# A decode block on one core: K of the last pair ahead of the projection, PV between the projection and its sums, and the last spread of O on GpSimd

## The chip, the cores and the metric

The kernel runs on one core of one Trainium2 chip. The metric is the device time of one execution in microseconds (us), as the median of several executions.

Engines are named as in the profile: PE is TensorE (PEld its weight loads), DVE is VectorE, ACT is ScalarE, POOL is GpSimd, SP is SyncE, which issues the loads.

## The reference

```python
def _A_ref(x, k_cache, v_cache, wq, wo):            # B=2, one token, D=512, 32 heads, 8192 keys, Dh=128
    q = (x @ wq) ...                                 # per head
    scores = jnp.einsum("bhqd,bhkd->bhqk", q, k) * (Dh ** -0.5)
    p = _softmax(scores, axis=-1)
    o = jnp.einsum("bhqk,bhkd->bhqd", p, v)
    return o.reshape(B, Sq, Hq * Dh) @ wo

h  = x + _A_ref(_layernorm(x), A_k_cache, A_v_cache, A_wq, A_wo)
h2 = h + _B_ref(_layernorm(h), W_gate, W_up, W_down)  # gated feed-forward, F=1376
```

Nearly all of the time goes into reading the two caches: 281 MB of bf16.

## The kernel before

The 64 (batch, head) items are handled as 32 pairs. For each pair a 4 MB block of K and a 4 MB block of V are loaded. The scores of a pair are shared out: VectorE does three quarters of a pair's scores (one multiply of 12288 elements per partition, four halving adds, one reduction), and TensorE the other quarter (transposes, a copy by ScalarE, small matmuls). TensorE then does PV. Pairs 0 to 29 run in a loop of 15 rounds; pairs 30 (`P0`) and 31 (`P1`) form the tail.

When a round's two heads are done, their output O is scaled by VectorE and *spread* over a padded tile by five small instructions, so that TensorE can *gather* it into the layout that the projection with `wo` needs. In the loop GpSimd spreads; for the last round before the tail, VectorE does.

```python
def o_spread(g, prog, *t_oc):
    e = prog.eng
    prog.wait(tok("og", g), *t_oc)
    if g >= 1:
        p0, p1 = ...
        prog.run(e.memset(O_l[:, :, :, p0:min(p1 + NM, 128)], 0.0))     # only writes
        prog.last()
    for a in range(2):
        p0, off = first(2 * g + a)
        n = min(NM, 128 - p0)
        e.tensor_copy(out=rsel[:, a, :], in_=rows[:, DR - off:2 * DR - off])   # reads SBUF
        i = e.tensor_tensor(out=O_l[:, a, :, p0:p0 + n], in0=O_cur..., in1=mask..., op=ALU.mult)  # reads SBUF
    i.then_inc(l2p, 1)

# TensorE, tail
collect(tail, 1)
k_part(tail, P0, (2, 3, 4, 5), ((k2p, 1),))            # K of pair 30: transposes and scores
nc.tensor.wait_ge(l2p, 1)                              # O spread
o_gather(tail)                                         # 4 matmuls
nc.tensor.wait_ge(a2p, 7)                              # ScalarE has copied the gathered O
nc.tensor.wait_ge(sem_wo, 16)
for r in range(DR):                                    # the projection: 30 matmuls 128x512
    i = nc.tensor.matmul(Op[1][32 * (r % 4):32 * (r % 4) + B, :], lhsT=O_all[:, r, :], rhs=X[:, r * D:(r + 1) * D], ...)
tail.mark("op", i)
nc.tensor.wait_ge(a2p, 9)                              # ScalarE has copied the projection
for c in range(DC):                                    # its sums, fp32
    nc.tensor.matmul(Wp[:, c * B:(c + 1) * B], lhsT=os_sb[:]..., rhs=sel2[:], ...)
k_part(tail, P1, (10, 11, 12, 13), ((k2p, 2),))        # K of pair 31
pv(tail, P0, ((JC, J, ((slot_sem[1], 16), (a2p, 6))), (0, JC, ((a2p, 8),))))   # 32 matmuls 128x512
pv(tail, P1, ((V_LAST, J, ...), (0, V_LAST, ...)), lambda: tail.mark("z", z_sum(Sp[0])))

# VectorE, in the pass over the pairs
if p >= P0:
    nc.vector.wait_ge(g2d, p - P0 + 1)
    nc.vector.wait_ge(slot_sem[s], 16)
    nc.vector.sem_inc(k2p, 1)
    dve.last()
    t_dm[p] = dve.run(k_mult(p))
    k_adds(p, dve.run, dve.last)
    ...
    t_s[p] = dve.run(k_reduce(p))
    if p == P0:
        dve.wait(t_ob_loop)
        normalize(Ob, dve.run, dve.last)
        o_spread(g - 1, dve, dve.run(o_scale()))
```

The softmax here doesn't subtract the row's maximum and nothing guards it: scores larger than these inputs give would overflow.

## Time and profile before

| what | number | view |
|---|---|---|
| time | 660.52 us (3 runs, 660.38 to 660.69) | the times |
| DMA in the chain of waits | 76% of the span | page, part 4 |
| DMA in the slices | 0.9 or more from the second slice to the last but one, mean 427 GB/s | page, part 2 |
| gather to end of PV, on the chain | 628.16 to 648.02, 19.86 us | chain of waits |
| last matmul of the feed-forward ends | 656.74 | chain of waits |
| last weights landed | 656.06 | landing records of the trace |

The chain of waits follows the end of the execution backward to what released each step. These are its pieces of the tail (start, duration, engine, tile, line of the kernel):

```profile
628.16 0.30 PE O L431 x4
...
628.78 3.60 PE O L463 x30
...
633.05 2.03 PE W L469 x8
635.08 0.97 PE T L381 x4
...
641.12 6.01 PE O L405 x54
...
648.04 0.61 ACT os_sb L569
```

From the gather (L431) the path goes through the projection (L463), a wait of 0.67 us for ScalarE's copy of it, the sums (L469), K of pair 31 (from L381 at 635.08 to 641.12), and PV of both pairs (L405).

GpSimd's timeline in the loop (start, duration, instruction, shapes):

```profile
592.28 0.21 POOL L525 COPY rsel<-rows 128x30 bf16<-128x30 bf16 x1
...
592.90 0.30 POOL L537 COPY q_c<-q_all 128x136 bf16<-128x136 bf16 x1
604.09 3.48 POOL L537 COPY q_c<-q_all 128x136 bf16<-128x136 bf16 x1 [10.89 <-DVEq L591]
```

The same copy of q took 0.30 us beside VectorE's reduction and 3.48 us when it started with VectorE's first add (604.05 to 607.42).

The last load and its issue, from the list of DMA issues (size, us to landing) and SyncE's timeline. First the list:

```profile
wd_last<-in_B_W_down_dram SPq DMA_DIRECT2D x1, 96.0 KB, 27.8
```

```profile
628.22 2.39 SPq L706 DMA_DIRECT2D wd_last<-in_B_W_down_dram  x1
```

Issued at 628.2 and landed 27.8 us later: 656.1, only 0.7 us before the last matmul that needs it ends. All these loads go through one queue (281.06 of the 281.17 MB).

### The profile page before, as it was taken

The page shows a single profiled execution, that of the slowest core. Times are in us where ns is not written, and L with a number is a line of the kernel's source. Part 1 is how long each engine was busy: PE and PEld are TensorE (multiplying, and loading weights), DVE is VectorE, ACT ScalarE, POOL GpSimd, SP SyncE. Part 2 cuts the span into 40 slices and gives each one's busy share as a digit, 9 for nine tenths or more (in the row PEclk, how much of TensorE's full clock was granted, in tenths as well). Part 3 has the DMA queues.
Part 4 walks back from the last instruction along what each step waited for, and adds up shares of the span by engine and source line. Part 5 has one row for each costly group of instructions (what it writes and reads, how often), then busy time and mean ns, then how long its engine had stood idle before and what let it go on. Part 6 is the DMA issues. An engine that isn't in the chain of part 4 may idle for free.

```text
span 659.2 us, 7582 instructions
## 1 busy us (share of the span) xinstructions
PE 324.3 (49%) x3073; PEld 188.6 (29%) x3073; DVE 469.2 (71%) x280; ACT 213.6 (32%) x431; POOL 73.5 (11%) x125
## 2 busy tenths in 40 slices
PE   2753454435455343655535364443556444354577
PEld 0331332213233121433313142221324222133344
DVE  1585576788767678776768877676886767787991
ACT  1622333143342223334223343422324332333250
POOL 3002002020200202020020201002020110202000
PEclk9856556565756657555665756756555765655656
DMA  8999999999999999999999999999999999999997
GB/s 366 444 437 431 420 445 416 443 428 431 438 422 441 422 439 433 428 435 424 441 422 439 433 428 433 426 441 422 439 434 426 435 424 441 424 437 433 428 417 295
DMA packets 10653, 281.17 MB, mean 427 GB/s; under 512 B 1202, under 2 KB 1300, under 8 KB 1812
## 3 DMA queue, kind: packets, MB, share of 16 engines
q1 hardware_dynamic: 10632, 281.06, 99.3%
q8 instruction: 5, 0.08, 0.1%
q14 instruction: 4, 0.03, 0.0%
q10 hardware_dynamic: 12, 0.00, 0.0%
HBM read 281.05 MB, written 0.00 MB: 426 GB/s over the span
## 4 chain that ended last, share of the span: by engine, by line
DMA 76%; DVE 19%; PE 4%; issue 1%; ACT 1%; SPq 0%; DVEq 0%
DMA slot<-in_A_k_cache_dram 76%; DVE prod L540 16%; DVE prod L549 2%; PE O L405 1%; PE O L463 1%; PE T L381 0%; ACT kT L566 0%; PE W L469 0%; DVE scores L554 0%; PE S L756 0%; PE O L756 0%; PE O L808 0%; PE Ob L417 0%; SPq L172 0%; PE S L364 0%
## 5 line engine op out<-in xcount | busy, mean ns | idle before, releaser
L540 DVE TENSOR_TENSOR prod<-slot,q_c 128x12288 bf16<-128x12288 bf16 x32 | 209.9, 6558 | 148.0 <-DMA slot<-in_A_k_cache_dram 141.3
L405 PE MATMUL O<-slot,e 128*16 128x512 bf16 x1024 | 119.3, 621 | 219.9 <-ACT e L495 146.2
L549 DVE TENSOR_TENSOR prod<-prod 128x6144 bf16<-128x6144 bf16 (+3 forms) x128 | 212.2, 1657 | 7.8
L566 ACT ACTIVATE kT<-T 128x1024 bf16<-128x1024 bf16 x128 | 126.1, 1022 | 144.6 <-PE T L381 141.9
L381 PE MATMUL T<-ident_f,slot 128*128 128x128 f32 x512 | 108.6, 365 | 29.1 <-DVEq L587 29.1
L405 PEld LDWEIGHTS O<-slot,e 128*16 128x16 bf16 x1024 | 26.4, 114 | 287.0 <-ACT e L495 172.9
L495 ACT ACTIVATE e<-scores 64x96 bf16<-64x96 f32 x64 | 19.5, 304 | 239.6 <-DVEq L601 238.9
L381 PEld LDWEIGHTS T<-ident_f,slot 128*128 128x128 f32 x512 | 79.0, 188 | 44.2 <-DVEq L587 43.3
L537 POOL COPY q_c<-q_all 128x136 bf16<-128x136 bf16 x32 | 57.2, 1788 | 195.5 <-DVEq L591 152.5
L364 PE MATMUL S<-q_c,kT 128*128 128x4 bf16 x1024 | 47.4, 168 | 40.8 <-ACT kT L566 40.0
L364 PEld LDWEIGHTS S<-q_c,kT 128*128 128x128 bf16 x1024 | 39.1, 104 | 67.9 <-ACT kT L566 66.8
L417 PE MATMUL Ob<-sel,os_sb 128*128 128x4 f32 x136 | 30.1, 345 | 24.2 <-ACT os_sb L569 24.2
L417 PEld LDWEIGHTS Ob<-sel,os_sb 128*128 128x128 f32 x136 | 28.6, 311 | 26.1 <-ACT os_sb L569 26.1
L520 POOL MEMSET O_l<- 128x40 bf16 (+1 forms) x13 | 1.8, 136 | 303.9 <-DVEq L598 303.9
L554 DVE TENSOR_REDUCE scores<-prod 128x96 f32<-128x768 bf16 x32 | 30.5, 953 | 2.8
L566 ACT ACT_TABLE_LOAD x15 | 19.2, 1283 | 0.3
L495 ACT ACTIVATE e<-S 64x32 bf16<-64x32 f32 x64 | 13.0, 202 | 15.1 <-PE S L364 14.7
L569 ACT ACTIVATE os_sb<-O 128x512 f32<-128x512 f32 x17 | 10.1, 597 | 12.8 <-PE O L405 12.4
L495 ACT ACTIVATION_READ_ACCUMULATOR e<-S 64x1 f32 x64 | 12.8, 201 | 0.7
L495 ACT ACTIVATION_READ_ACCUMULATOR e<-scores 64x1 f32 x64 | 11.8, 185 | 0.0
L426 PEld LDWEIGHTS Ob<-zs,ones_f 128*128 128x128 f32 x30 | 7.1, 296 | 12.5 <-issue 12.5
L525 POOL COPY rsel<-rows 128x30 bf16<-128x30 bf16 x28 | 5.9, 209 | 33.3 <-DVEq L598 32.5
(104 smaller groups left out, 90.6 us busy)
## 6 DMA issues: line engine op xcount, KB each, us to landing
slot<-in_A_k_cache_dram SPq DMA_DIRECT2D x32, 4096.0 KB, 32.1
slot<-in_A_v_cache_dram SPq DMA_DIRECT2D x31, 4096.0 KB, 30.3
slot<-in_A_wq_dram SPq DMA_DIRECT2D x1, 4096.0 KB, 12.2
X<-in_A_wo_dram SPq DMA_DIRECT2D x1, 3840.0 KB, 45.8
slot<-in_A_v_cache_dram SPq DMA_DIRECT2D x1, 3072.0 KB, 23.3
slot<-in_B_W_up_dram SPq DMA_DIRECT2D x1, 1376.0 KB, 23.2
slot<-in_B_W_gate_dram SPq DMA_DIRECT2D x1, 1376.0 KB, 26.2
slot<-in_A_v_cache_dram SPq DMA_DIRECT2D x1, 1024.0 KB, 25.4
```

The costliest lines, as they stand in the source:

```text
L364: i = nc.tensor.matmul(Sp[p % 2][:, 2 * jj:2 * jj + 4], lhsT=kv_[:, k, r, :], rhs=q_c[p % 2][:, 4 * r:4 * r + 4], start=(r == 0), stop=(r ...
L381: i = nc.tensor.transpose(Tp[g % 2][:, k * 128:(k + 1) * 128], k_t[:, j:j + 2, :].rearrange("p j d -> p (j d)").bitcast(F32), ident_f[:])
L405: i = nc.tensor.matmul(Op[0][c:c + 16, :], lhsT=e_t[q][:, j // VJ, :], rhs=v_t[:, j:j + VJ, :].rearrange("p j d -> p (j d)"), start=(q == ...
L417: i = nc.tensor.matmul(Ob[:, 0:4], lhsT=os_sb[:, jj * Dh:(jj + 1) * Dh], rhs=sel[:, 4 * jj:4 * jj + 4], start=(jj == 0), stop=(jj == VJ - 1))
L426: return nc.tensor.matmul(bank[:, ZC:ZC + 8], lhsT=ones_f[:], rhs=zs[:], start=True, stop=True)
L495: i = nc.scalar.activation(out=e_t[q][h, j0 // VJ:j1 // VJ, 8 * q:8 * q + 8].rearrange("p g (j a) -> p g j a", a=2)[:, :, :, a], in_=src(h ...
L537: nc.gpsimd.tensor_copy(out=q_c[p % 2][:], in_=q_all[:, p]).then_inc(g2d, 1)
L540: return nc.vector.tensor_tensor(out=prod[:, 0:JC, :], in0=tile((2 * p) % 4)[:, 0:JC, :], in1=q_c[p % 2][:, 8:QW].unsqueeze(1).broadcast_t ...
L549: run(nc.vector.tensor_tensor(out=prod[:, 0:JC, 0:w], in0=prod[:, 0:JC, 0:w], in1=prod[:, 0:JC, w:2 * w], op=ALU.add))
L554: return nc.vector.tensor_reduce(out=scores[p % PG][:, 0:JC], in_=prod[:, 0:JC, 0:8], axis=AX.X, op=ALU.add)
L566: to_pe(nc.scalar.activation(out=kT[gg % 2][:], in_=Tp[gg % 2][:].bitcast(BF16), func=ACT.Copy))
L569: to_pe(nc.scalar.activation(out=os_sb[:], in_=Op[0][:], func=ACT.Copy))
```

## The change

Its intent: K of pair 31 fills the time in which TensorE would wait for the spread, PV of pair 30 fills the time in which ScalarE copies the projection, and VectorE is rid of the spread. ScalarE's instructions are put in the matching order.

```diff
                 k_part(tail, P0, (2, 3, 4, 5), ((k2p, 1),))
+                k_part(tail, P1, (7, 8, 9, 10), ((k2p, 2),))
                 nc.tensor.wait_ge(l2p, 1)
                 o_gather(tail)
-                nc.tensor.wait_ge(a2p, 7)
+                nc.tensor.wait_ge(a2p, 12)
 ...             (the projection)
-                nc.tensor.wait_ge(a2p, 9)
+                pv(tail, P0, ((JC, J, ((slot_sem[1], 16),)), (0, JC, ((a2p, 13),))))
+                nc.tensor.wait_ge(a2p, 14)
 ...             (its sums)
-                k_part(tail, P1, (10, 11, 12, 13), ((k2p, 2),))
-                pv(tail, P0, ((JC, J, ((slot_sem[1], 16), (a2p, 6))), (0, JC, ((a2p, 8),))))
                 pv(tail, P1, ...)
 ...
                             normalize(Ob, dve.run, dve.last)
-                            o_spread(g - 1, dve, dve.run(o_scale()))
+                            t_oc = dve.run(o_scale())
 ...
+                        if p == P0:
+                            o_spread(g - 1, pool, t_oc)
 ...             (ScalarE: O_all, exp of pair 30's VectorE part and os_sb move behind K of pair 31)
```

## The prediction

> **What bounds it now.** The page says DMA is 76% of the chain of waits. Only the tail after the loop can change. There the chain of waits, in order of time, runs: VectorE finishes pair 30 (reduction ends 627.0 us), scales O (627.5) and spreads it (five instructions, to 628.1); TensorE gathers (0.3), ScalarE copies (0.25), the projection takes 3.60, its copy 0.61, its sums 2.03, K of pair 31 6.0, PV of pairs 30 and 31 with the z sums 6.9, to 648.02. The feed-forward part follows and its last matmuls end at 656.74. Close behind lie the loads: the last quarter of V of pair 31 is there at 645.9, the gate weights at 652.5, the last down weights at 656.07. So nothing done in the tail can gain more than about 0.4 us: whatever TensorE saves, the last down matmuls wait for 656.07.
>
> **What the change does.** K of pair 31 (6.0 us) leaves the path between gather and result, and stands where TensorE would have to wait for the spread anyway, at about 627.6 (its K landed at 626.4; the release comes from VectorE when pair 30 is scaled). PV of pair 30 (3.3) covers the copy of the projection (0.7). Were the spread still ready at about 628.5, TensorE would run K to 633.6, gather, project to 638.3, PV 30 to 641.7, sums to 643.7, PV 31 to about 647.2: 0.8 us sooner, of which the loads leave 0.4.
>
> **What it costs.** The spread goes to GpSimd, and VectorE's next instruction is now pair 31's multiply (6.56 us), directly followed by adds of 3.36, 1.77, 0.97 and 0.57. The timeline of GpSimd in the loop shows the danger: the copy of q (128x136) takes 0.30 when VectorE runs a reduction, and 3.48 when it starts with VectorE's first add (604.09 to 607.57; the add ends at 607.42). The Trainium skill, "SBUF — State Buffer", section "Who interferes with whom", says it: a VectorE instruction with two SBUF inputs contends with a GpSimd instruction that reads SBUF, and the later one is fully blocked. The loop's own spreads took 0.15 us apiece only because they fall beside a reduction (592.1 to 593.0). Here they fall beside the multiply. The memset only writes and should pass. The four reading instructions should each get through at one gap of VectorE: about 634.1 (end of the multiply), 637.5, 639.3, 640.3. So O is spread at about 640.4 instead of 628.1.
>
> TensorE then idles from about 633.6 to 640.5. From the gather to the end of PV it took 19.9; without K (6.0) and the copy's wait (0.7) it takes 13.15: 653.6 instead of 648.0, an estimate. The rest (8.7 us to the last matmul) stands. So +5.5 us.
>
> **Predicted:** 665.8 us, range 660.0 to 667.5 (8 in 10). Faster by over 2%: 0.005; within 2%: 0.985; slower by over 2%: 0.01.
>
> **What would show it.** GpSimd's last copies and products last microseconds each and end at VectorE's boundaries, the last near 640.4; TensorE waits about 7 us before the gather; K of pair 31 runs at 627.6 to 633.6; the projection starts near 641; loads land as before.
>
> **What would make it wrong.** If GpSimd gets all four instructions through in the first gap (634.1 to 634.9), the tail ends as before, 660.5 or so. If it isn't blocked at all, 660.1. If GpSimd misses gaps, O comes at the latest with the reduction, near 641.3: 666.8.

## The result, and the profile after

The changed kernel took 660.62 us (median of 6 runs, 660.17 to 661.04); the kernel before, in the same rounds and the first ones, 660.57 (6 runs, 660.14 to 660.69). The ratio is 1.0002, with a 95% interval of 0.9989 to 1.0015: the same. A ratio here is the mean time of one kernel's fast runs over that of the other's of the same rounds, so it is not quite the ratio of the medians quoted.

The predicted 665.8 was wrong by 5.2 us. The chain of waits of the changed kernel in the same stretch:

```profile
627.45 0.17 DVE O_cur L510
...
627.88 6.39 POOL rsel L525
634.27 0.17 POOL O_l L526
634.43 3.28 POOL rsel L525
637.71 0.17 POOL O_l L526
...
637.93 0.30 PE O L431 x4
...
638.55 3.58 PE O L464 x30
642.12 1.81 PE O L405 x31
643.93 1.96 PE W L471 x8
645.89 1.40 PE O L405 x24
647.29 0.32 PE S L426 x2
647.61 0.57 PE O L405 x8
...
648.20 0.61 ACT os_sb L569
```

VectorE's timeline there has pair 31's multiply (to 634.20) and, from 634.24, its four adds:

```profile
627.64 6.56 DVE L540 TENSOR_TENSOR prod<-slot,q_c 128x12288 bf16<-128x12288 bf16 x1
634.24 6.83 DVE L549 TENSOR_TENSOR prod<-prod 128x6144 bf16<-128x6144 bf16 x4
```

GpSimd is now on the chain. Its spread took 10.2 us instead of 0.55, and the gather started 9.8 us later (637.93 instead of 628.16). And yet PV ended at 648.18, where it had ended at 648.02. From the gather to the end of PV, TensorE took 10.25 us in place of 19.86. Of these 9.6 us, 6.0 are K of pair 31 and 0.7 the wait for the copy, both as planned. The remaining 2.9 were not planned: PV itself (64 matmuls and the z sums, those of the softmax weights) took 4.1 us of the chain (1.81 + 1.40 + 0.32 + 0.57) instead of 6.9 (641.12 to 648.02). The view of stretches shows why (us; busy time and number of instructions of each engine; granted clock of TensorE; DMA share; GB/s). Before:

```profile
core 0: us, PE busy (x) PEld busy (x) DVE busy (x) ACT busy (x) POOL busy (x), PEclk, DMA share, GB/s
...
641.80:645.20 3.40, 3.40 (x36) 1.17 (x32) 0.52 (x1) 0.94 (x5) 0.00 (x0) 0.50 1.01 423
645.20:648.60 3.40, 2.79 (x30) 0.84 (x22) 0.34 (x2) 0.56 (x1) 0.00 (x0) 0.74 1.03 434
```

After:

```profile
641.80:645.20 3.40, 3.40 (x40) 2.06 (x32) 0.25 (x1) 1.35 (x5) 0.00 (x0) 0.95 1.00 417
645.20:648.60 3.40, 2.95 (x37) 1.52 (x37) 0.34 (x2) 0.40 (x1) 0.00 (x0) 1.00 1.03 433
```

Before, PV ran at a granted clock of 0.50 until 646.9. After, the clock was 1.00 from 642.2 on. The weights landed at 656.12 (656.06 before).

So two things needed an explanation: why the spread was ready at 637.9 and not at 640.4, and where the full clock came from.

### The profile page after: what moved, and what is told of

The parts are those of the page before. It is cut to its first block, busy times and chain, and to the rows that moved or that the text cites. A ratio compares the mean times of both kernels' runs of the same rounds, so it can differ in the third digit from the quotient of the medians.

```text
span 659.2 us, 7580 instructions
## 1 busy us (share of the span) xinstructions
PE 324.4 (49%) x3072; PEld 191.0 (29%) x3073; DVE 469.1 (71%) x275; ACT 213.6 (32%) x431; POOL 82.8 (13%) x130
## 4 chain that ended last, share of the span: by engine, by line
DMA 76%; DVE 18%; PE 3%; POOL 2%; issue 1%; SPq 0%; DVEq 0%; ACT 0%
DMA slot<-in_A_k_cache_dram 76%; DVE prod L540 16%; DVE prod L549 2%; POOL rsel L525 1%; PE O L405 1%; PE O L464 1%; PE W L471 0%; DVE scores L554 0%; PE S L758 0%; PE O L758 0%; PE O L810 0%; SPq L172 0%; PE Ob L417 0%; ACT os_sb L569 0%; DVEq L587 0%
## 5 line engine op out<-in xcount | busy, mean ns | idle before, releaser
L405 PE MATMUL O<-slot,e 128*16 128x512 bf16 x1024 | 117.4, 610 | 219.5 <-ACT e L495 146.3
L381 PE MATMUL T<-ident_f,slot 128*128 128x128 f32 x512 | 110.8, 371 | 29.2 <-DVEq L587 29.2
L381 PEld LDWEIGHTS T<-ident_f,slot 128*128 128x128 f32 x512 | 80.6, 191 | 44.2 <-DVEq L587 43.3
L525 POOL COPY rsel<-rows 128x30 bf16<-128x30 bf16 x30 | 15.6, 519 | 33.4 <-DVEq L598 32.5
L569 ACT ACTIVATE os_sb<-O 128x512 f32<-128x512 f32 x17 | 10.1, 597 | 12.7 <-PE O L405 12.4
L495 ACT ACTIVATION_READ_ACCUMULATOR e<-S 64x1 f32 x64 | 12.8, 201 | 0.7
L426 PEld LDWEIGHTS Ob<-zs,ones_f 128*128 128x128 f32 x30 | 7.2, 299 | 12.8 <-issue 12.8
```

The lines of the kernel that those rows point to most:

```text
L381: i = nc.tensor.transpose(Tp[g % 2][:, k * 128:(k + 1) * 128], k_t[:, j:j + 2, :].rearrange("p j d -> p (j d)").bitcast(F32), ident_f[:])
L405: i = nc.tensor.matmul(Op[0][c:c + 16, :], lhsT=e_t[q][:, j // VJ, :], rhs=v_t[:, j:j + VJ, :].rearrange("p j d -> p (j d)"), start=(q == ...
L495: i = nc.scalar.activation(out=e_t[q][h, j0 // VJ:j1 // VJ, 8 * q:8 * q + 8].rearrange("p g (j a) -> p g j a", a=2)[:, :, :, a], in_=src(h ...
L569: to_pe(nc.scalar.activation(out=os_sb[:], in_=Op[0][:], func=ACT.Copy))
```

## The experiments

Fourteen runs were made, two of them repeats of the two kernels: the first eight for both questions and the limit set by the loads, four more when the first theory of the clock fell, and two to test the next one. "PV ends" is read from the timelines and chains, "full clock from" from the clock records in the traces, which are multiples of 3.41 us long.

### The spread: who holds up whom

**hold_multiply** lets VectorE's multiply wait until GpSimd has spread O.

```diff
                         nc.vector.sem_inc(k2p, 1)
+                        if p == P1:
+                            nc.vector.wait_ge(l2p, 1)
                         dve.last()
```

> The changed kernel, but VectorE's multiply of pair 31 waits until GpSimd has spread O. Theory (the port held by the multiply and the first add stretched the spread): all five GpSimd instructions take 0.15 to 0.21 us, the spread is ready near 628.6, the multiply starts near 628.7 and the gather follows K of pair 31 directly. Rival (GpSimd is slow by itself here): the first copy still takes microseconds.

Measured (one look, 660.16 us): the five instructions took 0.15 to 0.21 us each, as in the loop. GpSimd's timeline:

```profile
627.60 0.15 POOL L520 MEMSET O_l<- 128x44 bf16 x1 [19.98 <-DVE O_cur L510]
627.82 0.21 POOL L525 COPY rsel<-rows 128x30 bf16<-128x30 bf16 x1
...
628.29 0.21 POOL L526 TENSOR_TENSOR O_l<-O_cur,mask 128x10 bf16<-128x10 bf16 x1
```

Against 6.39 and 3.28 us for the two copies in the changed kernel, this shows that VectorE's multiply and first add held them up. The memset is as fast with the multiply beside it (0.16). That is what the Trainium skill, "SBUF — State Buffer", section "Who interferes with whom", says of instructions that only write, and of reading ones beside a VectorE instruction with two SBUF inputs.

**copies_first** puts both copies ahead of both products.

```diff
+                    for a in range(2 * copies_first):
+                        off = first(2 * g + a)[1]
+                        e.tensor_copy(out=rsel[:, a, :], in_=rows[:, DR - off:2 * DR - off])
                     for a in range(2):
 ...
-                        e.tensor_copy(out=rsel[:, a, :], in_=rows[:, DR - off:2 * DR - off])
+                        if not copies_first:
+                            e.tensor_copy(out=rsel[:, a, :], in_=rows[:, DR - off:2 * DR - off])
```

> The changed kernel with the order of GpSimd's instructions changed: both copies of rows first, then both products. Theory two per gap (any two short reading instructions pass in one gap between VectorE's instructions): first copy held to the end of the multiply, 634.2, second copy passes with it in 0.2 us, first product is held for the first add to 637.6, second product passes. Rival by kind (copies are held, products aren't, since they follow a copy): second copy held to 637.6, both products short after it. Ready near 637.9 either way; the durations decide.

Measured (one look, 660.49 us), GpSimd's timeline (two instructions to a line):

```profile
628.03 6.53 POOL L524 COPY rsel<-rows 128x30 bf16<-128x30 bf16 x2
634.52 3.48 POOL L530 TENSOR_TENSOR O_l<-O_cur,mask 128x12 bf16<-128x12 bf16 x2
```

Both copies are done 0.2 us after the multiply ends (634.35), both products 0.2 us after the first add. So it isn't the kind that counts: two short reading instructions pass at each boundary between VectorE's instructions.

**early_copies** does the memset and both copies before O is scaled, so that only the two products come after it.

```diff
-                    prog.wait(tok("og", g), *t_oc)
+                    prog.wait(tok("og", g), *(() if hoist else t_oc))
 ...
+                    if hoist:
+                        for a in range(2):
+                            off = first(2 * g + a)[1]
+                            e.tensor_copy(out=rsel[:, a, :], in_=rows[:, DR - off:2 * DR - off])
+                        prog.wait(*t_oc)
```

> The changed kernel with the memset and both copies of the spread done ahead of VectorE's scaling (they need only the gather of the round before), so that only the two products follow it. Two per gap: both held to the end of the multiply, ready near 634.5, before K of pair 31 is done; the gather then comes near 635, and by the clock theory the end of PV stays at 648.0 to 648.8 and the time within 0.5 us of before. Products never held: ready near 628.2. One per gap: near 637.8. Rival of fixed durations: 0.4 us faster.

Measured: 660.36 us (660.19 to 660.69, 4 runs) beside 660.34 of before, ratio 0.9999 (0.9982 to 1.0016). Both products passed at the end of the multiply:

```profile
627.82 6.74 POOL L532 TENSOR_TENSOR O_l<-O_cur,mask 128x12 bf16<-128x12 bf16 x2 [18.20 <-DVE O_cur L510]
```

The gather came at 634.61, 3.3 us earlier than in the changed kernel. PV ended at 647.38, only 0.8 us earlier (by the timeline), because TensorE needed 12.8 us: the full clock lasted here only from 640.8 to 644.2. The rule of two per boundary held in the three orders tried (the changed kernel, copies_first, early_copies).

### The parts of the change, and the limit of the loads

**spread_only** is the kernel before with the spread alone moved to GpSimd.

```diff
-                            o_spread(g - 1, dve, dve.run(o_scale()))
+                            t_oc = dve.run(o_scale())
 ...
+                        if p == P0:
+                            o_spread(g - 1, pool, t_oc)
```

> The kernel before with the spread alone moved to GpSimd, in the old order. All theories: the spread is ready near 637.9, TensorE idles from 627.4 to then, K of pair 31 still to do after the projection. With the lock and fixed durations at half clock (19.9 us from the gather): PV ends at 657.8, time 670.3. With the clock paid back (over 10 us idle): gather to end of PV takes 16 to 17 us, PV ends near 654.5, time 666 to 668.

Measured: 669.58 us (669.05 to 670.5), ratio 1.0146 (1.0129 to 1.0163). The gather came at 638.06; TensorE had idled for 10.2 us. The full clock came only at 654.5. The result lies between the two forecasts and nearer to fixed durations at half clock: ten idle microseconds had not brought the clock back for the projection, the sums or K.

**order_only** is the changed kernel with the spread back on VectorE.

```diff
-                            t_oc = dve.run(o_scale())
+                            o_spread(g - 1, dve, dve.run(o_scale()))
 ...
-                        if p == P0:
-                            o_spread(g - 1, pool, t_oc)
```

> The change with the spread back on VectorE. Theory (idle TensorE time is paid back as granted clock): the gather comes right after K of pair 31, near 635, 3 us earlier than in the changed kernel, TensorE never idles, stays at half clock, and needs about 13 us from the gather to the end of PV: end at 648.0 to 648.8, time within 0.5 us of both kernels. Rival (TensorE's work has fixed durations, 10.25 us from the gather as in the changed kernel's profile): PV ends near 646, held by the last V, and the time falls by about 0.4 us, to the floor that the last weights set.

Measured: 660.28 us (660.2 to 660.4), beside 660.23, ratio 1.0002 (0.9985 to 1.0018). The gather came at 634.75, PV ended at 646.58, and the idle theory was wrong here: without an idle stretch the full clock began at 638.8. TensorE's timeline now shows waits for loads:

```profile
643.39 1.47 PE L405 MATMUL O<-slot,e 128*16 128x512 bf16 x24 [0.43 <-DMA slot<-in_A_v_cache_dram]
644.80 0.39 PE L426 MATMUL S<-zs,ones_f 128*128 128x8 f32 x2
645.97 0.61 PE L405 MATMUL O<-slot,e 128*16 128x512 bf16 x8 [0.79 <-DMA slot<-in_A_v_cache_dram]
...
652.52 1.71 PE L756 MATMUL O<-d_b,slot 128*128 128x2 bf16 x44 [0.58 <-DMA slot<-in_B_W_gate_dram]
```

PV was 1.4 us ahead of the kernel before, but the end of the span was only 0.3 us ahead (658.84 against 659.18). The loads took the rest back.

**less_work** leaves out 22 of the 30 projection matmuls and 24 of the 32 PV matmuls of pair 30. Its output is wrong, which doesn't matter for the time. (The comparison with the reference isn't sensitive to these terms.)

```diff
-                for r in range(DR):
+                for r in (*range(4), *range(DR - 4, DR)):
 ...
-                pv(tail, P0, ((JC, J, ((slot_sem[1], 16),)), (0, JC, ((a2p, 13),))))
+                pv(tail, P0, ((JC, J, ((slot_sem[1], 16), (a2p, 13))),))
```

> Wrong result on purpose: the changed kernel with 22 of the 30 projection matmuls and 24 of the 32 PV matmuls of pair 30 left out, 3 to 5 us of TensorE time at half clock. Theory (the last weights land at 656.1 and set the floor): the end comes at most 0.5 us sooner, the time is 660.0 to 660.3, and TensorE waits for the last loads of V, the gate or the down weights. Rival (the tail is bound by TensorE's work): the time falls by 2 us or more.

Measured: 660.67 us (660.17 to 661.26, 4 runs), ratio 1.0008 (0.9991 to 1.0024). The median gained nothing at all, less than expected. In the profiled run, at the low end of the four, TensorE waited 1.13 us for the last V, PV of pair 31 ran at half clock (2.74 us for 24 matmuls where order_only took 1.47), and the chain of waits ended in the loads:

```profile
627.06 28.85 DMA slot<-in_B_W_down_dram
655.91 0.04 issue
655.95 0.56 PE O L810 x10
```

So the tail can't end sooner than the loads allow, even with the work of 46 matmuls less. This also hinted at the next section: with less to do, TensorE lost the full clock.

### The clock: a theory that fell

The first theory was that the idle 2.9 us before the gather had earned the full clock.

**fill_wait** fills that wait with 28 matmuls that nobody reads.

```diff
                 k_part(tail, P1, (7, 8, 9, 10), ((k2p, 2),))
+                nc.tensor.wait_ge(sem_wo, 16)
+                for n in range(28):
+                    c = 32 * (n % 4)
+                    nc.tensor.matmul(Tp[0][c:c + 16, :], lhsT=ident[:, 0:16], rhs=X[:, 0:D], start=True, stop=True)
                 nc.tensor.wait_ge(l2p, 1)
```

> The changed kernel with 28 idle-filling matmuls (128x512, into a bank that is free, never read) in the stretch where TensorE waits for GpSimd's spread (about 2.9 us at half clock). Theory: without the idle stretch the clock stays at half, gather to end of PV takes about 13 us instead of 10.25, PV ends near 651, and the time rises by 2 to 3 us, to 662.5 to 663.7. Rival (the clock has nothing to do with the idle stretch): PV ends at 648.2, the time stays at 660.6.

Measured: 660.32 us (660.24 to 660.37), ratio 1.0001. The theory's 662.5 or more did not come. Full clock began at 641.7 and PV ended at 647.9. In the profiled execution K of pair 31 ended at 633.4 and not at 635.1 as in the changed kernel's profile, so 1.4 us of the wait stayed unfilled; TensorE idled for half as long as in the changed kernel (2.9) and got the clock just the same.

**late_gather** puts an idle stretch into order_only by hand.

```diff
                 nc.tensor.wait_ge(l2p, 1)
+                nc.tensor.wait_ge(late, 1)
                 o_gather(tail)
 ...
                         last()
+                        if p == NP - 1 and w == Dh // 4:
+                            nc.vector.sem_inc(late, 1)
```

> order_only with an idle stretch put back by hand: TensorE waits before the gather until VectorE has done the first add of pair 31 (about 638.2), though O was spread at 628. Theory: the idle 3 us bring back the full clock, PV ends at 648.0 to 648.8, and the time is within 0.5 us of order_only though the gather is 3 us later. Rival (fixed durations): PV ends 3 us later than in order_only, the time rises by 2.5 to 3 us.

Measured: 661.54 us (660.34 to 662.27), ratio 1.0016 (0.9999 to 1.0033). The gather came 3.6 us later than in order_only (638.34) and PV ended 2.9 us later (649.50). The idle stretch was not made up. The time rose by only 1.3 us because order_only had been waiting for loads.

**fill_loop** fills TensorE's 13 us wait in every round of the loop, in case low use over a longer time earned the clock.

```diff
                     nc.tensor.sem_inc(l2p, -1)
+                    for n in range(110):
+                        c = 32 * (n % 4)
+                        nc.tensor.matmul(Tp[0][c:c + 16, :], lhsT=ident[:, 0:16], rhs=q_all[:, 0:4, 8:QW],
+                                         start=True, stop=True)
                     pv(body, 1, ...)
```

> The changed kernel with 110 matmuls (128x512, into a free bank, never read) in each round of the loop, in the 13 us in which TensorE waits for the odd pair's V. Theory (little use of TensorE in the tens of microseconds before the tail earns the full clock that shortened the tail): the clock stays at half throughout the tail, gather to end of PV takes 13 us, PV ends near 651, the time rises by 2 to 3 us, to 662.5 to 664. Rival (the grant does not answer to what TensorE did): as the changed kernel, 660.2 to 661.1. The loop itself stays bound by the loads.

Measured: 661.14 us (660.82 to 661.48), ratio 1.001 (0.9994 to 1.0027). Full clock began at 644.2, and gather to end of PV took 11.2 us. Neither forecast was met exactly, but the half clock throughout that the theory asked for did not come; the mean granted clock over the span even rose to 0.70, from 0.59 before.

**after_again** and **before_again** are the two kernels once more, unchanged.

> The changed kernel once more, for the clock records of a second execution. If the grant follows from the program, the full clock begins near 642 again and lasts 10 us, gather to end of PV 10.25 us. If it varies between executions, the full clock falls elsewhere and this stretch takes up to 13 us, while the spread on GpSimd has the same durations (6.4, 0.2, 3.3, 0.2).

> The kernel before once more. In its first profile the gather to the end of PV took 19.9 us, all but 1 us of it at half clock. If the grant follows from the program, the same; if it varies between executions, 17 to 20 us, with the full clock elsewhere; the end is held by the last weights, 656.1, in any case.

Measured (one look each). The changed kernel: full clock from 643.3 (642.2 the first time), gather to end of PV 10.7 us (10.25), the spread with the same 6.38, 0.21, 3.33 and 0.20 us; 661.04 us. The kernel before: full clock from 645.7 (646.9), gather to end of PV 19.3 us (19.9); 660.42 us. So the exact place varies between executions, but by a microsecond or so, while the two kernels differ clearly.

**gather_640** is the changed kernel with the gather held until VectorE's third add, where the prediction had put the end of the spread. Its edit is that of late_gather with `Dh // 16`.

> The changed kernel with the gather held until VectorE has done its third add of pair 31, 640.3 to 640.5, where the prediction had put the end of the spread; the spread itself is untouched (ready near 637.9). If the time hangs on the gather microsecond for microsecond, it rises by 2 to 2.6 us over the changed kernel, to about 663; with TensorE at half clock to the end of PV, as the prediction assumed, it would be 665.8; if a later gather is made up by the clock, 660.6 to 661.2.

Measured: 663.43 us (663.07 to 664.24), ratio 1.0049 (1.0032 to 1.0066). The gather came at 640.79, 2.86 us later than in the changed kernel; the time rose by 2.8 over the changed kernel's median (it lies 3.2 above the kernel before of the same rounds). Gather to end of PV took 10.4 us; full clock began at 645.3. This weighs the two errors: a spread as late as predicted would have cost about 2.8 us. The rest of the miss, 2.4 us (665.8 − 663.4), is left for the clock; that is a remainder and not a measurement of its own.

### The clock: the theory that held

Put side by side, the traces show another pattern. Full clock begins 2.7 to 5.9 us after the start of an unbroken run of 128x512 matmuls (projection, PV):

| kernel | run of 128x512 matmuls starts | full clock from |
|---|---|---|
| before | projection alone 628.78; PV 641.05 | none; 646.9 |
| before, again | projection alone 630.06; PV 642.33 | none; 645.7 |
| spread_only | projection alone 638.69; PV 650.95 | none; 654.5 |
| after | projection and PV of 30: 638.55 | 642.2 |
| after, again | 638.81 | 643.3 |
| order_only | 636.09 | 638.8 |
| early_copies | 635.23 | 640.8 |
| late_gather | 638.94 | 644.5 |
| gather_640 | 641.39 | 645.3 |

The other traces of the first twelve runs fit: hold_multiply 634.90 and 640.6, copies_first 638.68 and 641.9, fill_wait 638.59 and 641.7 (after its fill), fill_loop 638.54 and 644.2, less_work 643.56 (PV of pair 31 alone) and 646.8.

The Trainium skill, "TensorE: Matmul & The Clock Gate", section "What's actually happening", says it: the default is half clock, and a busy window of about 3.4 us, in windows that run freely, releases it. Under this theory the projection alone (3.6 us) seldom fills such a window; joined to PV of pair 30 it makes a run of about 7 us at half clock, which always does. The part of the change that was meant to hide a wait of 0.7 us would then have earned the clock. Two more runs tested this.

**sums_first** undoes only that part: PV of pair 30 stands after the sums again.

```diff
-                pv(tail, P0, ((JC, J, ((slot_sem[1], 16),)), (0, JC, ((a2p, 13),))))
                 nc.tensor.wait_ge(a2p, 14)
 ...             (the sums)
+                pv(tail, P0, ((JC, J, ((slot_sem[1], 16),)), (0, JC, ((a2p, 13),))))
                 pv(tail, P1, ...)
```

> The changed kernel with one of its parts undone: PV of pair 30 stands after the sums of the projection again, so that TensorE's run of 128x512 matmuls is 3.6 us of projection, then a wait and the sums, then 6.9 us of PV. Theory (the full clock comes after an unbroken run of such matmuls that fills one of the 3.41 us windows in which the records count; 3.6 us seldom does, 7 us always does): the full clock begins in the PV stretch, 3.4 to 6.8 us after its start near 644.5, not near 642; gather to end of PV takes 12 to 14 us, the time rises by 1.5 to 3.5 us over the changed kernel, to 662.2 to 664.2. Rival (the clock falls where it falls, or answers to the wait): full clock from 641 to 645 as in the changed kernel, only the 0.7 us wait for the copy comes back, 660.9 to 661.4.

Measured: 662.76 us (661.39 to 664.59), ratio 1.0039 (1.0018 to 1.0061), 2.1 us more than the changed kernel's median and 2.4 more than the kernel before of the same rounds. The stretches:

```profile
638.40:641.80 3.40, 3.07 (x32) 0.95 (x31) 3.30 (x4) 0.99 (x5) 0.00 (x0) 0.50 0.98 419
641.80:645.20 3.40, 2.71 (x22) 2.13 (x20) 0.56 (x1) 1.34 (x5) 0.00 (x0) 0.98 0.99 414
645.20:648.60 3.40, 3.40 (x40) 1.23 (x36) 0.00 (x0) 0.00 (x0) 0.00 (x0) 0.52 1.00 422
```

Here the projection alone did earn one stretch of full clock, from 641.9 to 645.3. I had not expected it; it is where the rival had put the full clock. It was spent on the wait and on the fp32 sums, which took 2.03 us at either clock, and was lost again as PV began. PV then had to earn it anew, from 648.8. Gather to end of PV took 12.4 us (638.24 to 650.64). Of the 2.15 us more than in the changed kernel, 0.7 is the wait for the copy and most of the rest PV's slower matmuls. The rival had asked for 661.4 at most.

**long_fill** is fill_wait with 44 matmuls instead of 28, so that the run of 128x512 matmuls starts earlier.

```diff
+                nc.tensor.wait_ge(sem_wo, 16)
+                for n in range(44):
+                    c = 32 * (n % 4)
+                    nc.tensor.matmul(Tp[0][c:c + 16, :], lhsT=ident[:, 0:16], rhs=X[:, 0:D], start=True, stop=True)
                 nc.tensor.wait_ge(l2p, 1)
```

> The changed kernel with 44 filling matmuls (128x512, into a free bank, never read) in front of the gather instead of the 28 of an earlier run, so that TensorE runs such matmuls from the end of K of pair 31 (633.4 to 635.0) nearly up to the gather, over 4.5 us. Theory: together with the projection the run is long enough that the full clock begins between 637 and 641.5, earlier than in the changed kernel (642.2 and 643.3 in two executions); part of the projection runs at full clock, gather to end of PV takes 8.5 to 10 us, the time is 660.2 to 661. Rival (no link to the run of matmuls): full clock from 642 to 645, gather to end of PV 10.2 to 11.2 us.

Measured: 660.35 us (660.08 to 660.49), ratio 1.0001 (0.9985 to 1.0018). Full clock from 638.2, 4.9 us after the fill began at 633.29. TensorE's timeline:

```profile
633.29 4.87 PE L462 MATMUL T<-X,ident 128*16 128x512 bf16 x44
...
638.70 1.89 PE L468 MATMUL O<-X,O_all 128*2 128x512 bf16 x30 [0.33 <-ACT O_all L679]
```

The projection took 1.89 us instead of 3.58, and gather to end of PV 8.6 us. Doing more work made the rest faster; as in order_only, the loads kept the gain.

long_fill came out as the theory asks and not as its rival. sums_first did so in its time and in PV's clock, but not in the clock right after the projection.

**Where the windows lie.** The traces settle that difference. The clock records of an execution lie on one grid of 3.41 us. Cut each of the sixteen executions along its own grid, from 624 us on, and add up in each window how long TensorE was in 128x512 matmuls. (This was read off afterwards; no run was made to test it.) All 17 half-clock windows with 2.8 us or more were followed by full clock, none of the 92 with 2.5 us or less was, and of two with 2.7 one was. The projection alone was split over two windows in the kernel before (1.09 and 2.49 us), in its repeat (2.03 and 1.55) and in spread_only (2.16 and 1.41); in sums_first nearly all of it fell into one (3.06). So where the grid happens to lie decides for the projection alone, while a run of 7 us contains a whole window in any case. Full clock stayed after every window with 1.47 us or more and went after every one with 1.35 us or less. So it went in early_copies at 644.2, although TensorE had been busy for 3.30 of the 3.41 us: 1.34 were 128x512 matmuls, most of the rest the fp32 sums.

No version tried is faster than the kernel before, so there is none to recommend over it.

## Why the prediction was wrong

- **The bound by the loads: right.** It said that nothing done in the tail gains more than about 0.4 us. order_only ended PV 1.4 us sooner and the span 0.3; less_work cut 46 matmuls and gained nothing.
- **GpSimd blocked by the multiply and the adds: right.** The copies took 6.39 and 3.28 us, and 0.21 each in hold_multiply. (K of pair 31 ended at 635.1, not at 633.6, but the gather waited for the spread and not for K.)
- **"The four reading instructions should each get through at one gap of VectorE": wrong in size.** Two get through at each boundary. The spread was ready at 637.9, not 640.4, and TensorE waited 2.9 us before the gather, not 7. gather_640 measured what the later gather would have cost: about 2.8 us.
- **"Without K (6.0) and the copy's wait (0.7) it takes 13.15": wrong in size.** It took 10.25, because the sum used durations that PV had at half clock in the profile before. The change joined the projection and PV of pair 30 into one long run of 128x512 matmuls and so brought the full clock forward. sums_first, which separates the two again, took 12.4 us and cost 2.1 us, 0.7 of it the wait for the copy. In the traces the term was 2.9 us too long (13.15 − 10.25).
- Of the 5.2 us between 665.8 and 660.6, the first error thus makes up 2.8 and the second the remaining 2.4. 660.62 lies just inside the low end of the stated range, but the forecast of a clear slowdown failed. That it is also close to the 660.5 named for "all four instructions in the first gap" is chance: two passed there, two at the next, and the clock made up the rest.
- **What became of the gain:** the spread on GpSimd gave the gather 9.8 us later (alone it costs 9.4 us, spread_only). Moving K of pair 31 ahead (6.0), the hidden copy (0.7) and the clock (2.9) paid 9.6 of that back. The new order without the slow spread (order_only) is no faster, as the loads end at 656.1 to 656.4 in every case.

What stays open: the exact share of a window that the full clock needs, which lies here between 2.5 and 2.8 of 3.41 us, and what else counts. fill_wait's shorter fill fits (1.5 and 1.7 us in its two windows). But earlier in the sixteen executions (25 to 624 us) 77 of the 225 starts of full clock followed windows with less than 2.5 us of 128x512 matmuls, which other matmuls had filled, fp32 transposes above all, so these matmuls are not the whole rule.

## What to carry to other kernels

A duration read at half clock is not a property of the matmul: when a change moves matmuls together or apart, ask whether the new run is long enough to earn the full clock, and what stands in between that loses it. Small GpSimd instructions that read SBUF belong beside VectorE's reductions, or ahead of its long two-input instructions; behind the start of one, each pair of them waits for a whole VectorE instruction. And before tuning the tail of a kernel that is bound by loads, look up when the last load lands: that is all there is to gain.

## What the Trainium skill lacked or had wrong

- "SBUF — State Buffer", "Who interferes with whom": it says that the later instruction is fully blocked, which the runs confirm, but not what happens at the boundary. Two short reading GpSimd instructions (128x30 and 128x12) pass there, the second within 0.2 us, and VectorE pays little: its four adds took 6.83 us in the changed kernel and 6.73 in the kernel before.
- "TensorE: Matmul & The Clock Gate", "What's actually happening": confirmed in kind (full clock 2.7 to 5.9 us after a run of 128x512 matmuls starts, in pieces of 3.41 us). It doesn't say how busy a window must be: a projection of 3.6 us alone brought no full clock in three executions (before, before again, spread_only: at most 2.49 us of it in one window) and one stretch of it in a fourth (sums_first: 3.06). Nor does it say how busy a window must be to keep it: here 1.47 us of 128x512 matmuls did, and 1.35 did not.
- On the same page the spacing of matmuls halves with the full clock, and PV's nearly did, from 0.111 us apiece (54 in 6.01) to 0.058 (24 in 1.40). But the eight fp32 matmuls that sum the projection took 2.03 us at both clocks, while the eight fp32 matmuls into Ob took 1.05 us at full clock and 1.87 at half (early_copies). No page that was read says which fp32 matmuls gain; the cause was not tested.
